# An mLSTM cell and a squared-ReLU FFN on one core: output gates loaded five chunks ahead instead of four

## The chip, the cores and the metric

The kernel runs on one core of a Trainium2 chip. The metric is the device time in microseconds of one execution, as the median of several runs. The engines are named as in the profile: PE (TensorE, with its weight loads PEld), DVE (VectorE), ACT (ScalarE), POOL (GpSimd) and SP (SyncE, which here only issues DMAs). Each engine takes its instructions in the order of the program, and waits for the others by semaphores.

## The reference, cut to what matters

An mLSTM cell runs over 768 steps for 4 batches and 8 heads of 40 elements. Its output, gated by the sigmoid of `o_gate`, is laid out as 3072 tokens of 320 and goes through an FFN.

```
for t in range(S):
    m_new  = maximum(f_gate[t] + m, i_gate[t])
    f_stab = exp(f_gate[t] + m - m_new);  i_stab = exp(i_gate[t] - m_new);  m = m_new
    C = f_stab * C + i_stab * outer(v[t], k[t])
    n = f_stab * n + i_stab * k[t]
    denom = maximum(abs(n . q[t]), 1)
    y[t] = sigmoid(o_gate[t]) * (C @ q[t]) / denom
x = y as (B*S, H*D) = (3072, 320)
h = maximum(x @ w_in, 0)            # 320 -> 2048
out = (h * h) @ w_out               # 2048 -> 320
```

The inputs, among them `o_gate` with its shape (4, 8, 768, 40), are float32.

## The kernel before

**Chunks and groups.** The sequence is cut into chunks of 128 steps: six to a batch, 24 in all, numbered s = 0 to 23. A chunk's attention is done at once for its eight heads: scores of keys and queries, weights from the decays, their product with the values, and a state C carried to the next chunk. Two chunks (256 tokens) make a group g of the FFN, 0 to 11. Both FFN layers are done for most groups with seven block products instead of eight, so that sums of blocks (`sums`, `sums_of_x`) come ahead of the products and sums of results (`ffn1_close`, `ffn2_fast`) after them.

**The order is written by hand.** The program is emitted in the order in which every engine works, without a planner. A prologue does chunks 0 to 5. Then a loop over `parts` (L1091) does the rest. Four parts, `at` = 0 to 3, go with each chunk s from 6 on, and each part holds a quarter of one FFN layer of one group: in the even ones from 8 on a second layer (`ffn2_fast`), in the odd ones from 9 to 25 a first layer (`ffn1_open`, `ffn1_close`). The attention of chunk s is spread over its four parts; after chunk 23 the parts hold only FFN work.

**A chunk's way through memory.** In part 1, `attend_turned(s)` leaves the numerators turned; `store_num(s)` writes them to a scratch tensor in HBM (`num_rows`, L580) and `load_num(s)` reads them back in another layout (four DMAs, L585). In part 2 `normalise_turned(s)` on DVE (L597 to L606) waits for them, takes the denominator, and multiplies by the gated output `og` of the chunk (L603 and L604 read it) into `x_sb`. Then, on SP: `store_rows(s)` writes `x_sb` out (L632), in odd chunks `load_A(s+2)` (L352), then `prefetch(s)`, then `load_rows(s)` reads the rows back turned (four DMAs, L637), then `pair_up(s+3)` (L305, four DMAs). All of these and the stores of the output (L801, L806) stand in SP's one queue.

**The output gates.** `load_o(s)` (L342) reads 160 KB of `o_gate` for chunk s into its place in a tile `og` that holds a run of chunks: (0, 1), (2, 3), and then four to a run: 4 to 7, 8 to 11, 12 to 15, 16 to 19, 20 to 23 (`RUNS`, L288). The pool has two such tiles, so a run's tile takes the buffer of the run before the last: 12 to 15 takes that of 4 to 7, 16 to 19 that of 8 to 11, and so on. It is opened by the load of the run's first chunk (L339, L340). `sigmoid(r)` (L345) works in place on ACT. To keep ACT from changing its table of functions often, the sigmoids come four at a time: in part 3 of every chunk with s % 4 = 3, for the next run (L1153 to L1156). Chunks up to 11 are loaded in the prologue.

**What stands behind the sigmoids on ACT.** In chunks 11, 15 and 19 part 3 goes on with `ffn1_close`, whose first ACT instruction is the relu L907. The next chunk's part 0 is `ffn2_fast(g, 0)`: PE makes a product into the bank X, and ACT copies it out as `m1` (L785). PE's part 1 goes on summing into the same bank X (L789), so it cannot start before this copy.

The loop's `do(f, s)` calls `f(s)` if 0 <= s < 24 (L923).

Of the kernel before, what the change touches and what calls it, by code (L numbers as in the profile page):

```python
# [29 lines left out]
def kernel(  # L30
# [305 lines left out]
    def load_o(s):  # L336
        b, c = divmod(s, NB)
        r, (s0, s1) = next((r, (a, z)) for r, (a, z) in enumerate(RUNS) if a <= s < z)
        if s == s0:  # L339
            st["og", r] = ld.tile([P, 4, H, D], F32, name="og")  # L340
        og = st.setdefault(s, {})["og"] = st["og", r][:, s - s0]
        nc.sync.dma_start(og, o_gate[b, :, c * P : (c + 1) * P, :].rearrange("h p d -> p h d"))  # L342
# [580 lines left out]
    def do(f, s):  # L923
        if 0 <= s < NT:
            f(s)
# [16 lines left out]
    def load_part(s, i):  # L942
        b, c = divmod(s, NB)
        dst, src = load_parts(s)[i]
        nc.sync.dma_start(dst, src[b, :, c * P : (c + 1) * P, :].rearrange("h p d -> p h d"))
# [65 lines left out]
    for u in range(8):  # L1011
        s = 2 + u // 2
# [72 lines left out]

    def prefetch(s):
        do(lambda s: load_part(s, 2), s + 4)
        if 8 <= s < 20:
            load_o(s + 4)

    for n, (which, g, i) in enumerate(parts):  # L1091
        s, at = 6 + n // 4, n % 4
# [80 lines left out]
        if at == 2:  # L1173
            do(lambda s: weigh(s, masked=True), s + 1)
            ffn1_square()
            if n < 4:
                do(turn_kq, s + 1)
                do(scale_q, s + 1)
            if even:
                do(weighted, s + 1)  # L1180
            do(normalise_turned, s)
            do(store_rows, s)
            if s < 7:
                do(load_squares, s + 2)
            else:
                if not even:
                    do(load_A, s + 2)
                prefetch(s)
            do(load_rows, s)
            if s > 6:  # L1190
                do(pair_up, s + 3)
            else:
                do(load_A, s + 2)
# [35 lines left out]
```

## Time and profile before

| what | value |
|---|---|
| median of 3 runs | 514.7 us |
| lowest and highest | 513.06 and 514.84 us |
| span of the profiled execution | 514.0 us |
| mean granted PE clock in it | 0.993 |
| ACT idle before `sigmoid`, until a load of `og` landed | 25.0 us in 3 times, the longest 8.8 |
| loads of `og` | 24 of 160 KB, 3.0 to 6.2 us from issue to landing, median 5.1 |

A line of a timeline gives the start in us from the begin of the span, the duration in us, the engine, the line of the kernel, the operation, the tile written and the tile read, the shapes and the count. In brackets stands how long the engine was idle before it and what ended that. A line of waits gives the engine and what it wanted to do, what it waited for, the total in us, how many times, and the longest. In the table of windows the columns are the stretch, its length, PE's busy time with the number of its instructions, the granted PE clock (1.00 is full speed), the busy share of the DMA engines, and GB/s. SPq is SP's queue of DMA issues: the duration of an issue is not that of the transfer.

### The profile page before, as it was taken

To read this page: it belongs to the slowest core of one execution; us is meant where nothing else is said; L and a number is where in the kernel's file an instruction comes from. 1 tells how busy PE (TensorE), PEld (TensorE's weight loads), DVE (VectorE), ACT (ScalarE), POOL (GpSimd) and SP (SyncE) were. 2 spreads that over 40 slices of the span, in tenths; PEclk is the share of its full clock that TensorE was granted. 3 is DMA by queue.
4 is the path that set the end of the run, shared out by engine and by line. 5 is a ranking of instruction groups with operands and counts; after the bars stand their busy time and mean duration, and the time that the engine had idled before them with its cause. 6 is when DMAs were issued, how large, how long until landed. Compare 5 with 4: busy or idle time off the path is not lost.

```text
span 514.0 us, 13827 instructions
## 1 busy us (share of the span) xinstructions
PE 497.0 (97%) x5640; PEld 460.1 (89%) x5641; DVE 351.5 (68%) x646; ACT 249.3 (49%) x492; POOL 119.9 (23%) x138
## 2 busy tenths in 40 slices
PE   9998989999999999989999989999979999999997
PEld 4867878897799999979999979999979999999997
DVE  8588948979956956647867666587576766645441
ACT  3767878853541650653551743551745550432400
POOL 3356723421332041013023005023004012020000
PEclk9999989999999999989999999999999999999999
DMA  9999897947566757666667677577575541210000
GB/s 190 212 229 205 257 199 141 219 94 144 125 129 149 157 122 145 143 149 127 133 145 146 128 159 150 124 159 148 122 154 117 112 119 49 72 17 27 1 27 26
DMA packets 238238, 67.74 MB, mean 132 GB/s; under 512 B 185600, under 2 KB 232704, under 8 KB 238176
## 3 DMA queue, kind: packets, MB, share of 16 engines
q1 hardware_dynamic: 238080, 66.68, 61.3%
q8 instruction: 44, 0.72, 0.6%
q10 hardware_dynamic: 96, 0.20, 0.1%
q14 instruction: 18, 0.15, 0.1%
HBM read 54.56 MB, written 17.86 MB: 141 GB/s over the span
## 4 chain that ended last, share of the span: by engine, by line
PE 81%; DMA 6%; DVE 6%; ACT 3%; SPq 2%; issue 1%; POOL 0%; DVEq 0%; POOLq 0%; ACTq 0%
PE h_ps L765 31%; PE h_ps L841 22%; PE h_ps L890 6%; PE h_ps L711 3%; DMA og<-in_o_gate_dram 3%; PE numT L551 3%; PE h_ps L674 3%; DMA num_rows<-tn 2%; PE hp L490 1%; SPq L585 1%; PE idle L934 1%; PE tp L453 1%; PE numT L542 1%; DMA kq<-num_rows 1%; PE tp L445 1%
## 5 line engine op out<-in xcount | busy, mean ns | idle before, releaser
L377 POOL TENSOR_SCALAR_AFFINE_SELECT A_bc<-A_bc 128x1024 f32<-128x1024 f32 x22 | 25.9, 1177 | 164.8 <-ACT kq L387 143.5
L765 PE MATMUL h_ps<-w_out,g 128*128 128x160 f32 x336 | 50.8, 309 | 4.2 <-ACT y_sb L785 4.2
L765 PE MATMUL h_ps<-T,S 128*128 128x160 f32 x352 | 51.6, 300 | 2.6 <-DVE g_c L909 1.5
L765 PEld LDWEIGHTS h_ps<-w_out,g 128*128 128x128 f32 x336 | 47.6, 195 | 5.8 <-ACT y_sb L785 4.5
L765 PEld LDWEIGHTS h_ps<-T,S 128*128 128x128 f32 x352 | 48.9, 190 | 3.3 <-issue 1.7
L401 ACT ACTIVATE A_bc<-A_bc,b_T 128x128 f32<-128x128 f32 x144 | 44.1, 388 | 7.0 <-POOL A_bc L377 6.7
L781 DVE TENSOR_TENSOR y_sb<-y_sb,h_ps 128x160 f32<-128x160 f32 x44 | 14.0, 319 | 46.2 <-PE h_ps L765 46.2
L871 ACT COPY r_sb<-h_ps 128x512 f32<-128x512 f32 x18 | 10.5, 585 | 71.3 <-PE h_ps L841 71.3
L841 PE MATMUL h_ps<-xT,w_in 128*128 128x128 f32 x320 | 42.8, 278 | 0.0
L841 PE MATMUL h_ps<-lent_t,w_in 128*128 128x128 f32 x320 | 42.2, 275 | 0.0
L841 PEld LDWEIGHTS h_ps<-xT,w_in 128*128 128x128 f32 x320 | 38.9, 192 | 1.1 <-issue 0.7
L890 PE MATMUL h_ps<-xT,w_in 64*64 64x128 f32 x960 | 39.4, 273 | 0.0
L841 PE MATMUL h_ps<-lent_t 128*128 128x128 f32 x320 | 39.1, 275 | 0.0
L841 PEld LDWEIGHTS h_ps<-lent_t,w_in 128*128 128x128 f32 x320 | 38.9, 192 | 0.0
L841 PEld LDWEIGHTS h_ps<-lent_t 128*128 128x128 f32 x320 | 37.3, 192 | 0.1
L890 PEld LDWEIGHTS h_ps<-xT,w_in 64*64 64x64 f32 x960 | 34.6, 133 | 2.4
L674 PE MATMUL h_ps<-xT,w_in 128*128 128x256 f32 x128 | 30.6, 392 | 1.2 <-POOL w_in L230 0.6
L568 DVE STREAM_TRANSPOSE tn<-numT 128x256 f32<-128x256 f32 x36 | 15.5, 444 | 22.8 <-PE numT L551 22.8
L765 PE MATMUL h_ps<-w_out,g_c 128*128 128x160 f32 x192 | 28.0, 302 | 1.5 <-ACT y_sb L785 1.5
L674 PEld LDWEIGHTS h_ps<-xT,w_in 128*128 128x128 f32 x128 | 24.3, 196 | 5.3 <-POOL w_in L230 1.0
L413 POOL TENSOR_TENSOR vw<-va,A_bc 128x328 f32<-128x328 f32 x15 | 13.4, 892 | 67.2 <-issue 47.0
L765 PEld LDWEIGHTS h_ps<-w_out,g_c 128*128 128x128 f32 x192 | 26.3, 190 | 2.2 <-ACT y_sb L785 1.6
(188 smaller groups left out, 1071.3 us busy)
## 6 DMA issues: line engine op xcount, KB each, us to landing
A_bc<-a_rows SPq DMA_DIRECT2D x22, 512.0 KB, 5.0
num_rows<-tn SPq DMA_DIRECT2D x18, 256.0 KB, 2.5
kq<-num_rows SPq DMA_DIRECT2D x72, 64.0 KB, 2.0
raw<-in_moe_w_out_dram SPq DMA_DIRECT2D x7, 640.0 KB, 4.1
kqT<-kq_rows SPq DMA_DIRECT2D x34, 128.0 KB, 3.2
kq<-in_k_dram SPq DMA_DIRECT2D x24, 160.0 KB, 3.7
va<-in_v_dram SPq DMA_DIRECT2D x24, 160.0 KB, 5.1
og<-in_o_gate_dram SPq DMA_DIRECT2D x24, 160.0 KB, 5.1
```

The lines of the kernel that those rows point to most:

```text
L377: nc.gpsimd.affine_select(A[:], A[:], compare_op=ALU.is_ge, fill=-1e30, base=0, pattern=[[0, H], [1, P]], channel_multiplier=-1,)
L401: nc.scalar.activation(d["W"][:, i * n + h, :], A[i][:, h, :], AF.Exp, bias=b_T[:, b, c, i * n + h : i * n + h + 1],)
L413: nc.gpsimd.tensor_tensor(d["vw"][:], d["va"][:], d["W"][:, :, P - 1 : P].to_broadcast([P, H, D1]), op=ALU.mult,)
L551: nc.tensor.matmul(numT[i][halves[g], e, :], lhsT=va_w[s % NKQ][:, h * D1 : h * D1 + DP], rhs=d["P"][h % 2][:, h // 2, :] if s < KQ_SQ els ...
L568: nc.vector.transpose(to[:, 2 * i : 2 * i + 2], numT[i][:, :2, :].rearrange("p c t -> p (c t)"))
L674: nc.tensor.matmul(hs[i][:, n, :], lhsT=w_in[:, a, fb * P : (fb + 1) * P], rhs=xT[:, :, a, :], start=(n == 0 and a == 0), stop=False,)
L711: nc.tensor.matmul(o_ps, lhsT=st["g2", g][:, fb, j * P : (j + 1) * P], rhs=w_out[:, fb, :], start=(fb == 0), stop=(fb == NF - 1),)
L765: nc.tensor.matmul(to, lhsT=lhsT[:, p], rhs=rhs[:, p, :], start=(start and p == 0), stop=(p == NPAIR - 1), skip_group_check=True,)
L781: add = lambda to, a, b: nc.vector.tensor_tensor(to, a, b, op=ALU.add)
L841: nc.tensor.matmul(to[:, n, :], lhsT=lhsT[:, 4 * q + n, :], rhs=rhs, start=(start and n == 0), stop=True, skip_group_check=True,)
L871: nc.scalar.copy(m1[:], X[:])
L890: nc.tensor.matmul(to[cols, n, :], lhsT=w_in2[rows, 4 * q + n, cols], rhs=rhs, start=(start and n == 0), stop=True, skip_group_check=True,)
```

## The change

`prefetch(s)` is called once in each chunk from 7 on, in part 2, between the store and the load of the chunk's rows. It loads the values for chunk s + 4. Before, it also loaded the output gates of chunk s + 4 in the chunks 8 to 19, so for chunks 12 to 23. After, it loads those of chunk s + 5 wherever there is such a chunk: called in chunks 7 to 18, for the same chunks 12 to 23. Nothing else changes: the sigmoids stay where they are, and so does the number of `og` tiles.

```diff
     def prefetch(s):
         do(lambda s: load_part(s, 2), s + 4)
-        if 8 <= s < 20:
-            load_o(s + 4)
+        do(load_o, s + 5)
```

## The prediction

> **What bounds the kernel now.** I read the page first: the busy row, then the chain that ended last, by engine and by line.
>
> ```profile
> PE 497.0 (97%) x5640; PEld 460.1 (89%) x5641; DVE 351.5 (68%) x646; ACT 249.3 (49%) x492; POOL 119.9 (23%) x138
> ...
> PE 81%; DMA 6%; DVE 6%; ACT 3%; SPq 2%; issue 1%; POOL 0%; DVEq 0%; POOLq 0%; ACTq 0%
> PE h_ps L765 31%; PE h_ps L841 22%; PE h_ps L890 6%; PE h_ps L711 3%; DMA og<-in_o_gate_dram 3%; PE numT L551 3%; PE h_ps L674 3%; DMA num_rows<-tn 2%; PE hp L490 1%; SPq L585 1%; PE idle L934 1%; PE tp L453 1%; PE numT L542 1%; DMA kq<-num_rows 1%; PE tp L445 1%
> ```
>
> PE is the bound, with 17 us of idle time in 514.0; so a gain is PE idle time removed, or PE made faster. The chain has the load of og in it with 3.2% (16.5 us). That is not the gain: while the chain runs through that load, PE works. What the load costs PE is in PE's own waits, taken from 96 us on (the loop of parts):
>
> ```profile
> PE h_ps L765 <- ACT y_sb L785: 5.7, 3, 2.5
> PE h_ps L765 <- DVE g_c L909: 1.5, 1, 1.5
> PE h_ps L765 <- DVE g L909: 1.2, 2, 0.7
> ```
>
> Three waits for the copy L785, 5.7 us, and three for L909, 2.7 us. The timelines of ACT and of SP around the first place (chunk 11) say why ACT is late:
>
> ```profile
> 212.06 1.28 ACT L345 ACT_TABLE_LOAD   x1
> 213.35 1.19 ACT L345 ACTIVATE og<-og 128x320 f32<-128x320 f32 x3
> 222.85 0.47 ACT L345 ACTIVATE og<-og 128x320 f32<-128x320 f32 x1 [8.31 <-DMA og<-in_o_gate_dram]
> 223.22 0.58 ACT L907 ACTIVATE g<-h_ps 128x512 f32<-128x512 f32 x1
> 223.70 0.28 ACT L785 COPY y_sb<-h_ps 128x160 f32<-128x160 f32 x1
> ```
> ```profile
> 197.07 1.06 SPq L342 DMA_DIRECT2D og<-in_o_gate_dram  x1
> ...
> 215.35 0.38 SPq L632 DMA_DIRECT2D x_rows<-x_sb  x1
> ...
> 217.03 0.82 SPq L342 DMA_DIRECT2D og<-in_o_gate_dram  x1
> ```
>
> Three sigmoids run at once; the fourth, og(15), is issued only at 217.03, lands 5.8 us later, and ACT stands 8.31 us with the relu L907 and the copy L785 behind it. PE at the three places (chunks 11, 15, 19):
>
> ```profile
> 224.04 6.20 PE L765 MATMUL h_ps<-w_out,g 128*128 128x160 f32 x32 [2.52 <-ACT y_sb L785]
> ...
> 303.39 4.61 PE L765 MATMUL h_ps<-w_out,g_c 128*128 128x160 f32 x32 [1.52 <-ACT y_sb L785]
> ...
> 381.56 4.61 PE L765 MATMUL h_ps<-w_out,g 128*128 128x160 f32 x32 [1.70 <-ACT y_sb L785]
> ```
>
> The same 32 products take 6.20 us at the first place and 4.61 at the others. The windows of PE show the reason, the granted clock (column after the busy time):
>
> ```profile
> 223.50:224.00 0.50, 0.00 (x0) 0.88 0.56 76
> 224.00:225.00 1.00, 0.96 (x4) 0.50 0.44 129
> ...
> 226.00:227.00 1.00, 1.00 (x6) 0.50 0.95 312
> 227.00:227.50 0.50, 0.50 (x5) 0.71 0.91 162
> 227.50:228.00 0.50, 0.50 (x6) 1.00 0.76 136
> ```
>
> Half clock for 3.4 us, right after the longest of the three gaps.
>
> **What the Trainium skill says.** "TensorE: Matmul & The Clock Gate", Part 1 (What's actually happening): PE's clock is halved after a window of about 3.4 us (3413 ns) with little activity, and the window runs freely, so whether a gap triggers it depends on its phase. The trace agrees in length (3.4 us at 0.50), and the shorter gaps of 1.52 and 1.70 us left the clock at 1.00. The same page (Architectural detail) calls ACT a strict FIFO; the trace agrees, L907 starting 0.37 us after the late sigmoid. "Perfetto Trace Analysis", DMA Instruction — HWDGE: an issue's duration leaves out the movement of data; here 0.82 us of issue against 5.8 us to landing.
>
> **The change part by part.** Before, prefetch(s) loads og(s+4); sigmoid(12..15) stands in chunk 11, part 3, one part after og(15) is issued; likewise chunks 15 and 19. After, og(15) is issued where og(14) was, at 197.07, and lands at about 202, ten microseconds before the sigmoids begin at 213.35.
>
> ACT: the fourth sigmoid follows the third at about 214.5, ends at 215.0, L907 (0.58) by 215.6, and L785 runs when its product ends (213.79 + 2.44 = 216.2), so by 216.6. PE wants that bank at 221.5 (224.04 - 2.52): 5 us to spare. At the other places the product ends at 295.9 and 373.1, PE comes at 301.9 and 379.9: the wait goes whole. PE saves 2.52 + 1.52 + 1.70 = 5.74 us. These lie on the bound engine with nothing beside them.
>
> Clock: without the 2.52 us gap the halved window at 223.9 has no cause: 6.20 - 4.61 = 1.59 us more. From below it is worth 0 (a run whose window fell otherwise); from above 1.7 (3.41 us at half clock). I take 1.6. A second such window, about 67 to 70.4 us (mean clock 0.84 from 60 to 70), lies before the loop; I leave it in.
>
> What PE meets next: the second product of the step writes the bank that DVE's L781 reads; L781 comes after L760, done at 221.17, so by 221.5, and PE needs it at 221.5 + 2.2. No wait. The three L909 waits hang on normalise_turned waiting for num_rows, not on og: they stay.
>
> SP: 12 loads before, in chunks 8 to 19; 12 after, in chunks 7 to 18, each at the same place in the queue. Only the ends differ. Chunk 7 gains an issue (0.65 median): SP waits there for 0.64 us anyway (va issued until 138.19, xT's load from 138.83, for x_rows to land), and later for DVE's L574 before L580, 1.6 us; 0. The 160 KB beside xT's loads may stretch these by up to 0.9 us (they take 4.0 there, 4.4 to 4.9 where og goes ahead): hidden by the same wait. Chunk 19 loses an issue of 0.82 us, before work with slack: 0, at best -0.9.
>
> New wait: in chunks 7, 11 and 15 the load opens a tile over the buffer of the run that ends in that very chunk, so it needs normalise_turned(s) to have read it. The last read, L604, ended at 214.6; SP's store of x_rows at 215.35, just ahead, has already waited for the later L606. So the wait is met on arrival; 0, or the 0.02 to 0.05 us that SP's small pieces take in the chain. Behind it stand four xT loads, pair_up's four and store_num(s+1); DVE's next normalise waits for the last.
>
> Sum: 5.74 + 1.59 = 7.3 us; 514.0 becomes 506.7 by the profiled span. The three timed runs give 514.7 in the middle, 0.7 more; with the same difference 507.4.
>
> **The rivals.**
> Only the gaps (0.20): the median run had no halved window at that place. The times speak for it a little (513.06 to 514.84, a spread of one such window), the profiled execution against. 514.7 - 5.74 = 509.0.
> Another wait takes part of it (0.07): store_num(12) follows pair_up on SP at 225.06 whatever PE does, so its rows do not come earlier. They land near 231.1 (229.1 + 2.0) and normalise(12) would start at 236.05 - 4.1 = 231.9: 0.8 us spare; in chunk 16, 313.05 against 314.85 - 1.5: 0.3 us. If DVE comes late there and PE's banks with it, half of 5.74 returns: 514.7 - 2.9 - 1.6 = 510.2. Against it: DVE's work there is not what PE waits for next.
> More (0.07): the early halved window (1.6) or part of the L909 waits (2.7) goes too, about 2.4 of the 4.3: 505.0.
> Nothing (0.02): the sigmoid waits for something else than the load that is moved; the wait's name speaks against it. 514.7.
> Slower (0.04): the reused buffer is given free not by L604 but by something in the next chunk, so SP stands in its queue in chunks 7, 11 and 15. It decides from about 5 us of hold (normalise(12) at 236.05 against rows at 231.1). A hold of 9 us, to L568 of the next chunk, costs 3 x 4 = 12 us against 7.3 gained: 519.4. Against it: L604 is the last reader that the code has.
> The forecast: 0.60, with its own range 506.2 to 508.6.
>
> **How the numbers follow.** The likeliest case gives 507.4. The range takes in the case of the gaps alone and most of the case of more: 505.5 to 510.0, leaving out half of those at either end, nothing and slower, under 0.2. A measurement of this kernel tells about 0.5%, 2.6 us, from no change. Faster by more: 0.60 + 0.20 + 0.07 + 0.07 = 0.94; within: 0.02; slower: 0.04.
>
> **What would show it.** Right: no idle time of ACT before og, L785 before 217, no wait of PE for L785, PE's 32 products at 4.6 us in chunk 12, clock 1.00 there, L909's waits as before, og no more in the chain. Wrong: SP idle before L342 in chunk 7, 11 or 15; a new PE wait in chunks 12, 16 or 20; or a halved window somewhere else in the loop, which gives the 1.6 us back.

## The result, and the profile after

| | before | after |
|---|---|---|
| median of 4 runs | 514.77 us | 508.12 us |
| lowest and highest | 513.06 to 514.97 | 507.12 to 508.66 |
| ratio, with its 95% interval | | 0.9876 [0.9848, 0.9904] |
| span of the profiled execution | 514.0 us | 506.9 us |
| mean granted PE clock in it | 0.993 | 0.997 |

The change made the kernel faster by 6.65 us; the forecast said 7.3 us less and 507.4. Ratios and intervals, here and below, leave out the executions that took over 1.5% longer than the fastest of their kernel. The page of the changed kernel, in the lines that answer to those shown of before:

```profile
PE 494.5 (98%) x5640; PEld 458.7 (90%) x5641; DVE 352.0 (69%) x646; ACT 250.0 (49%) x492; POOL 122.4 (24%) x138
...
PE 94%; DVE 2%; issue 1%; ACT 1%; DMA 1%; POOL 0%; SPq 0%; DVEq 0%; POOLq 0%
PE h_ps L765 34%; PE h_ps L841 25%; PE h_ps L890 8%; PE h_ps L674 4%; PE numT L551 4%; PE h_ps L711 3%; PE hp L490 2%; PE h_ps L445 2%; PE tp L445 2%; PE numT L542 1%; PE idle L934 1%; PE h_ps L685 1%; PE tp L453 1%; PE dC L483 1%; PE dC L561 1%
```

The load of og is gone from the chain, which is now 94% PE. PE's busy time fell by 2.5 us with the same 5640 matmuls, its idle time from 17.0 to 12.4 us. ACT's timeline at the end of chunk 11 shows the mechanism as forecast: four sigmoids in a row, no idle time ahead of them, and the copy L785 at 214.06 after a wait for its own product only.

```profile
211.15 1.55 ACT L345 ACTIVATE og<-og 128x320 f32<-128x320 f32 x4
212.60 0.57 ACT L907 ACTIVATE g<-h_ps 128x512 f32<-128x512 f32 x1
214.06 0.29 ACT L785 COPY y_sb<-h_ps 128x160 f32<-128x160 f32 x1 [0.88 <-PE h_ps L765]
```

PE's waits, again from 96 us on, are all new ones. Neither L785 nor L909 is among them:

```profile
PE h_ps L445 <- PE h_ps L765: 2.6, 3, 0.9
PE h_ps L445 <- issue: 1.6, 1, 1.6
```

L445 is the product of `scores(s+1)`, in part 1 of an even chunk; the four waits are in chunks 14, 16, 18 and 20 (0.93, 0.94, 0.74 and 1.60 us). The releasers named ("PE", "issue") are not the cause; what PE waits for is found on PE's and DVE's timelines. First PE, at the three places of the old waits or near them:

```profile
218.49 4.61 PE L765 MATMUL h_ps<-w_out,g 128*128 128x160 f32 x32
...
292.95 1.11 PE L445 MATMUL h_ps<-kqT 40*64 40x128 f32 x29 [0.94 <-PE h_ps L765]
...
370.07 1.23 PE L445 MATMUL h_ps<-kqT 40*64 40x128 f32 x29 [1.60 <-issue]
```

The 32 products in chunk 12 take 4.61 us instead of 6.20. But ahead of the scores there are now gaps, 0.94 us in chunk 16 and 1.60 in chunk 20. DVE's timeline just ahead of the second:

```profile
364.64 0.17 DVE L597 TENSOR_SCALAR dm<-kq 128x8 f32<-128x8 f32 x1 [4.34 <-DMA kq<-num_rows]
...
366.35 0.68 DVE L908 TENSOR_TENSOR r_sb<-r_sb,h_ps 128x512 f32<-128x512 f32 x1
...
368.74 1.24 DVE L334 STREAM_TRANSPOSE kqT<-kqT 128x1024 f32<-128x1024 f32 x1
```

DVE waited 4.34 us for the numerator rows of chunk 19 (`load_num`), then worked without a pause through `normalise_turned`, L908 to L911 and `turn_kq` (L334). That ends at 369.98, and PE starts `scores` on its result at 370.07. The windows of PE after the gap (columns as in the earlier table of windows):

```profile
370.00:371.00 1.00, 0.93 (x30) 0.97 1.14 261
371.00:374.00 3.00, 3.00 (x43) 0.50 0.76 112
374.00:374.50 0.50, 0.50 (x20) 0.65 0.11 20
374.50:375.00 0.50, 0.50 (x13) 1.00 0.55 154
```

Half clock again for 3.4 us (370.9 to 374.3), now in chunk 20.

**Where the time went, by the two profiles.** The loop, from the first numerator product of chunk 6 to the end, took 514.0 - 107.6 = 406.4 us before and 506.9 - 105.4 = 401.5 after: 4.9 us less. Of this 4.2 is idle time of PE (gaps over 0.1 us from 100 us on: 8.4 before, 4.2 after). The other 2.2 us of the 7.1 lie in the prologue, which the change does not touch; there before had the halved window near 67 us that the prediction had left in, and after had none. So the total agrees with the forecast better than its parts do. That is why both kernels were run again.

### The profile page after: what moved, and what is told of

It is laid out like the page before. It is cut to its first block, busy times and chain, and to the rows that moved or that the text cites. A ratio compares the mean times of both kernels' runs of the same rounds, so it can differ in the third digit from the quotient of the medians.

```text
span 506.9 us, 13821 instructions
## 1 busy us (share of the span) xinstructions
PE 494.5 (98%) x5640; PEld 458.7 (90%) x5641; DVE 352.0 (69%) x646; ACT 250.0 (49%) x492; POOL 122.4 (24%) x138
## 4 chain that ended last, share of the span: by engine, by line
PE 94%; DVE 2%; issue 1%; ACT 1%; DMA 1%; POOL 0%; SPq 0%; DVEq 0%; POOLq 0%
PE h_ps L765 34%; PE h_ps L841 25%; PE h_ps L890 8%; PE h_ps L674 4%; PE numT L551 4%; PE h_ps L711 3%; PE hp L490 2%; PE h_ps L445 2%; PE tp L445 2%; PE numT L542 1%; PE idle L934 1%; PE h_ps L685 1%; PE tp L453 1%; PE dC L483 1%; PE dC L561 1%
## 5 line engine op out<-in xcount | busy, mean ns | idle before, releaser
L765 PE MATMUL h_ps<-w_out,g 128*128 128x160 f32 x336 | 49.2, 303 | 0.0
L765 PEld LDWEIGHTS h_ps<-w_out,g 128*128 128x128 f32 x336 | 46.1, 190 | 1.4 <-issue 1.2
L387 ACT ACTIVATE kq<-A_bc 64x512 f32<-64x512 f32 x30 | 18.8, 626 | 18.8 <-DMA A_bc<-a_rows 18.6
L908 DVE TENSOR_TENSOR r_sb<-r_sb,h_ps 128x512 f32<-128x512 f32 x20 | 13.7, 684 | 20.7 <-PE h_ps L841 14.3
```

Source lines behind the costliest of these rows:

```text
L387: nc.scalar.activation(e[rows], st[s]["A"][0][rows, PR * i : PR * (i + 1), :], AF.Exp)
L765: nc.tensor.matmul(to, lhsT=lhsT[:, p], rhs=rhs[:, p, :], start=(start and p == 0), stop=(p == NPAIR - 1), skip_group_check=True,)
```

## The experiments

Each ratio is to the kernel before, run beside it on the same chip, since that median was 511.8 to 512.6 us in the later sets. The median is of all executions of a run. "L785" and "L445" are PE's waits so named from 96 us on, in the one profiled execution. Those of e4 and e11 took 511.66 and 514.26 us, long for their kernels, so their waits are less certain. The cuts of e4 and e7 are against the kernel before, all others against the changed kernel.

| run | median us | ratio, 95% interval | L785 | L445 |
|---|---|---|---|---|
| e1 before, again | 511.71 | 0.9983 [0.9963, 1.0004] | 5.4 | 0.4 |
| e2 after, again | 509.81 | 0.9933 [0.9904, 0.9961] | 0 | 4.3 |
| e3 last load only | 506.72 | 0.9879 [0.9833, 0.9924] | 0 | 1.6 |
| e4 sigmoid later | 508.63 | 0.9920 [0.9894, 0.9947] | 0 | 3.7 |
| e5 first run only | 510.31 | 0.9957 [0.9931, 0.9983] | 2.1 | 0.3 |
| e6 other runs only | 510.56 | 0.9954 [0.9932, 0.9976] | 2.2 | 3.2 |
| e7 PE kept busy | 512.44 | 0.9984 [0.9955, 1.0013] | 0.6 | 0.4 |
| e8 normalise late | 510.05 | 0.9952 [0.9928, 0.9976] | 0 | 4.2 |
| e9 pairs in even chunks | 505.29 | 0.9874 [0.9829, 0.9919] | 0 | 0.7 |
| e10 pairs in odd chunks | 508.35 | 0.9926 [0.9896, 0.9955] | 0 | 3.7 |
| e11 after, third time | 507.97 | 0.9920 [0.9902, 0.9938] | 0 | 5.3 |
| e12 values in even chunks | 504.45 | 0.9872 [0.9829, 0.9916] | 0 | 1.1 |

The runs e1 to e4, e5 to e8 and e9 to e11 were each made on one chip, e12 by itself. In e7 the added line shifts L785 to L786.

**e1 and e2: the two kernels unchanged.** What of the gain is there again on another chip?

> The kernel before once more, nothing changed, to see how many halved-clock windows each of its executions has. Each window takes 0.0033 off the mean granted clock (3.41 us at half speed in 514) and should add some 1.6 us. Theory A (windows come by chance, by the phase of the gaps): the executions differ in clock by steps of 0.0033 and in time by steps of 1.6 us; most have one in chunk 12 and one near 68 us, 514.7 in the middle. Rival (the windows belong to the kernel): clock 0.993 and the same time in all.

> The changed kernel once more. Theory A: 508.1 in the middle, clocks of 0.993 to 1.000 in steps of 0.0033, the higher the shorter the span. If the windows play no part in the spread, span and clock are not related.

The waits repeat: e1 has the three for L785 with 5.4 us, e2 has none and 4.3 us at L445 instead. The gain is smaller than in the first measurement: 0.9933, about 3.4 us, its interval just touching the first one's. The mean clock of an execution comes in steps of about 0.0033 (0.997, 0.993, 0.990, 0.987), and one stretch of 3.41 us at half clock in 510 us is such a step: 3.41 x 0.5 / 510 = 0.0033. Counted so, an execution has from none to five windows. On this chip the kernel before has 2.14 on average in the 22 executions of e1 and 2.48 in the 48 that ran beside all four runs, the changed kernel 2.50 in 18. Across the executions of a chip, the time rises by 1.15 ± 0.16, 1.48 ± 0.12 and 1.18 ± 0.20 us per window on the three chips. So the average price is somewhat below the 1.6 of the prediction, and no fall in the number can be seen.

This count has a weakness. The traces tell the place of each window, and of the 28 in the 14 profiled executions 21 lie at 40 to 74 us, in the prologue, which no run touches. In the loop there are seven: one in each of the two profiles of the kernel before, one in two of the three profiles of the changed kernel, one in e5 and two in e4. If these profiles are typical, the count says little of the loop, and the price is mainly that of a window in the prologue.

**e3: only the last load of each run.** Load og(15), og(19) and og(23) in chunks 10, 14 and 18; leave the others. That takes ACT's wait away with 3 loads moved in place of 12.

```diff
-        do(load_o, s + 5)
+        if 8 <= s < 20 and s % 4 < 3:
+            load_o(s + 4)
+            if s % 4 == 2:
+                load_o(s + 5)
```

> Only the last load of each run (og of chunks 15, 19, 23) goes one chunk earlier, into chunks 10, 14 and 18, behind the load that stands there; the other nine loads stay where they were. Theory A (the late landing of these three alone held ACT): no idle time of ACT before a sigmoid, no PE wait for L785, 508.1 as the changed kernel, within 1 us. Rival B (the order of the loads as a whole, or the issue added in chunk 7, matters): between 508 and 514.7. Doubling the issue in chunks 10, 14, 18 may cost SP 0.9 us each, which should be hidden.

It is faster than the changed kernel in the same set, 506.72 against 509.81. PE waits 1.6 us at L445 where e2 waits 4.3, and its loop takes 397.1 us against 400.2. So moving these three loads is enough for the benefit, and where SP has its loads matters for the rest: e3 takes the three out of odd chunks (11, 15 and 19) into even ones, while the change leaves six og loads in odd chunks as before.

**e4: the sigmoid later, the loads unmoved.** The fourth sigmoid goes into part 1 of the next chunk, behind the copies; no DMA is moved.

```diff
-                for r in range(s + 1, min(s + 5, NT)):
+                for r in range(s + 1, min(s + 5 if s < 11 else s + 4, NT)):
                     sigmoid(r)
...
             do(attend_turned, s)
+            if s > 11 and s % 4 == 0:
+                do(sigmoid, s + 3)
             do(decays, s + 1)
```

> All loads stay as in the kernel before (og(s+4)); instead the fourth sigmoid of the runs 12-15, 16-19 and 20-23 moves on ACT, from chunk 11, 15, 19 part 3 to chunk 12, 16, 20 part 1, behind the copy L785 and just ahead of the decays, where no further table load is needed. Theory A (the order on ACT is all that matters, the load itself hinders nobody): as the changed kernel, 508 to 509, no PE wait for L785, ACT idle before the fourth sigmoid at most about 1 us. Rival B (the gain comes from moving the loads): 514.7.

The ratio is 0.9920, as e11 has it for the whole change. The wait at L785 is gone, and 3.7 us come up at L445. The loads land late as before, but behind the copies they hold ACT up for little:

```profile
ACT og L345 <- DMA og<-in_o_gate_dram: 3.0, 3, 1.2
```

So the order on ACT is the cause of the old waits, and not the load as such. And the wait at L445 comes up here too, with all loads where they were: it is not made by the moved loads alone, it appears when PE gets there earlier.

**e5 and e6: one part of the change alone.** e5 moves the loads of og(12) to og(15), e6 those of og(16) to og(23).

```diff
 e5:
-        do(load_o, s + 5)
+        if s < 11:
+            load_o(s + 5)
+        elif 12 <= s < 20:
+            load_o(s + 4)
 e6:
-        do(load_o, s + 5)
+        if 8 <= s < 12:
+            load_o(s + 4)
+        if 11 <= s < 19:
+            load_o(s + 5)
```

> Only the loads of the run 12-15 go one chunk earlier (issued in chunks 7 to 10); those of 16 to 23 stay. Theory A: the PE wait for L785 of 2.5 us in chunk 12 goes and those of 1.5 and 1.7 us in chunks 16 and 20 stay; also the halved window that followed the longest gap: 2.5 to 4.1 us, 510.6 to 512.2. Rival C (each place only hands its time to the next): less than 1 us.

> Only the loads of the runs 16-19 and 20-23 go one chunk earlier (from chunk 11 on); those of 12 to 15 stay. Theory A: the waits of 1.5 and 1.7 us in chunks 16 and 20 go, the 2.5 us and its halved window in chunk 12 stay: 3.2 us, 511.5; with the run of place 1 the two gains sum to that of the whole change. What PE waits for behind normalise in chunks 15 and 19 stays and may show at L445 rather than at the product before it.

e5 gains 2.2 us (0.9 to 3.5 by its interval) and e6 2.4. The first place is worth about its gap of 2.52; a window's 1.6 on top, 4.1 in all, lies outside the interval. In e6 the wait at L445 comes up (3.2 us), as its expectation had it, in e5 hardly (0.3). Together the two are worth 0.0089, within what the whole change measured in its three sets (0.0067 to 0.0124). In e6 the first place keeps its wait, and its line on PE's timeline has the 32 products at full speed all the same:

```profile
222.49 4.61 PE L765 MATMUL h_ps<-w_out,g 128*128 128x160 f32 x32 [2.22 <-ACT y_sb L785]
```

No window at half clock follows it. So the 2.5 us of gap that the prediction called the window's cause makes one possible, not certain.

**e7: fill the gaps with work.** In the kernel before, the state products dC of chunks 12, 16 and 20 are done six, four and four times, with the same result, so that PE runs while it would wait.

```diff
+        for again in range({12: 6, 16: 4, 20: 4}.get(s, 1)):
             (the loop of dC products, indented)
```

> The kernel before, with PE's gaps of chunks 12, 16 and 20 filled: the 16 matmuls into dC are done six, four and four times (each pass about 0.41 us and with the same result), in the time in which PE would wait for L785. The waits stay as long in sum (gap and filling together), so no gain from them. Theory A (the halved window of chunk 12 comes from the idle time): clock 1.00 in chunk 12 in every execution, mean clock 0.997 to 1.000, about 1.6 us or less gained, 513 to 514. Rival (the window does not come from the gap): a window in chunk 12 as before, 514.7.

The windows are 1.77 on average against 2.09 of before in the same set, a difference of 0.32 ± 0.24, so that a fall is not shown; the profiled execution has none in the loop. The time, 0.9984 [0.9955, 1.0013], is not told from no change: 0.3 windows of 1.15 to 1.5 us would be 0.4 to 0.5 us, less than the interval can tell. What the gap's window is worth at this place stays open.

**e8: normalise behind L908 to L911.** If the wait at L445 came from DVE's order, with the transposition queued behind the late normalise, then the L908 group ahead of normalise should shorten it. The changed kernel, with `normalise_turned` and what follows it put behind `ffn1_close` in odd chunks:

```diff
-        if at == 2:
+        if at == (3 if fast and s > 8 else 2):
             do(normalise_turned, s)
```

> The changed kernel, and in the odd chunks from 9 on normalise_turned with all that follows it (the store and load of the rows, prefetch, pair_up) is emitted after ffn1_close of part 3 instead of before it, so that on DVE L908 to L911 stand ahead of the normalise, which waits about 4 us for num_rows. In the changed kernel PE waits 4.2 us in four places for the transpose L334 that stands behind these. Theory D (DVE's late turn_kq, held up by the wait for num_rows, is the rest of PE's idle time): the waits at L445 shrink, by up to 1.2 us each, 504 to 507. Rival (L334 waits for its own load, kqT): as the changed kernel, 508, or slower, since the rows go out 1.5 us later.

L445 stays at 4.2. Now the transposition has rows of its own to wait for:

```profile
DVE kqT L334 <- DMA kqT<-kq_rows: 7.5, 5, 1.9
```

Both the numerator rows and `kqT` come through SP's queue, one after the other. So a better order on DVE alone brings nothing here. The run does not acquit DVE's order by itself, since it also sends all that follows the normalise on SP out later; e9 and e12, which leave DVE's order as it is, show that the queue alone can take most of the wait away.

**e9 and e10: in which chunks SP has the loads.** e9 and e10 load two og at a time, e9 in even chunks, e10 in odd ones.

```diff
 e9:
-        do(load_o, s + 5)
+        if 8 <= s < 20 and s % 2 == 0:
+            load_o(s + 4)
+            load_o(s + 5)
 e10:
-        do(load_o, s + 5)
+        if s < 19 and s % 2:
+            load_o(s + 5)
+            load_o(s + 6)
```

> The same twelve loads, none of them in an odd chunk: the even chunks 8 to 18 load og(s+4) and og(s+5). Each load is issued at latest one chunk before its sigmoids, so PE should not wait for L785. Theory E (what PE still waits for at L445 in the changed kernel, 4.2 us, comes from SP's queue, which in the odd chunks has A_bc, va, og and xT in a row and is late with the next num_rows and kqT): the waits at L445 fall to 0 to 2 us, the loop from the first numT to the end takes 397 us or less, against 401.5 and 400.2 in the two profiles of the changed kernel; 505 to 507. Rival F (the waits come from the num_rows round trip itself, whatever else SP has to do): as the changed kernel, waits of 4 us.

> The other way round: all twelve loads in odd chunks, two in each of 7 to 17: og(s+5) and og(s+6). Again every load lands long before its sigmoid: no PE wait for L785. Theory E: SP is later by one more issue (0.8 to 2.2 us) in the odd chunks 9 to 17 and less loaded in 19; the waits at L445 grow to 5 to 9 us, so most of the change's gain is gone, 510 to 514. Rival F: as the changed kernel, waits of 4 us.

e9 waits 0.7 us at L445 and takes 505.29 us, 2.7 us less than the changed kernel in the same set (e11, 507.97). e10 was expected to have 5 to 9 us of the wait and has 3.7, no more than the changed kernel. The direction of e9 holds, the dose of e10 does not: a second load in the odd chunks does no further harm once the even ones have none. SP's timelines say in part why. From the store of the rows of an odd chunk (L632, chunks 11 to 17) to the next `store_num` it is 10.1 us on average in the changed kernel, 8.6 in e9 and 11.1 in e10; after the store of an even chunk (12 to 18) it is 9.9, 9.2 and 9.4. So e10 gets back in the even chunks half of what it loses in the odd ones, and the two together take 20.0, 17.7 and 20.5 us. That this sum decides fits the three kernels; it was not tested by itself.

**e11: the changed kernel once more**, beside e9 and e10.

> The changed kernel for the third time, beside the two variants on the same chip. Ratio to the kernel before between the two measured, 0.988 and 0.993; waits at L445 of about 4 us in sum, none for L785.

The ratio is 0.9920, a gain of 4.0 us, with no wait at L785 and 5.3 us at L445.

**e12: the same with another tensor.** The changed kernel, with the loads of the values va (of the same kind, on the same queue) taken out of the odd chunks. If SP's queue is the cause, it does not matter which load leaves it.

```diff
     def prefetch(s):
-        do(lambda s: load_part(s, 2), s + 4)
+        if s % 2 == 0:
+            do(lambda s: load_part(s, 2), s + 3)
+            do(lambda s: load_part(s, 2), s + 4)
         do(load_o, s + 5)
```

> The changed kernel (og loads in every chunk, odd ones too), but the loads of the values, 160 KB each as well, are taken out of the odd chunks: the even chunks 8 to 20 load va(s+3) and va(s+4). Theory E in the form that the runs so far leave (SP reaches store_num late in odd chunks because of what it has to issue before, whichever tensor it is): the issue of store_num in chunks 13, 15, 17, 19 comes at most 4 us after PE's last matmul into numT, instead of 4.6 to 5.4, and the waits at L445 fall from 4.2 to 0 to 2 us; 505 to 507. If it is the gates' own load, the waits stay at 4 us and the time at that of the changed kernel.

The median is 504.45 us, the ratio 0.9872, and PE waits 1.1 us at L445. SP's timelines in chunks 17 to 19 show how. First the changed kernel:

```profile
346.49 0.93 SPq L801 DMA_DIRECT2D out_dram<-y_sb  x1
347.51 0.39 SPq L632 DMA_DIRECT2D x_rows<-x_sb  x1
...
357.12 0.38 SPq L580 DMA_DIRECT2D num_rows<-tn  x1
...
360.20 2.90 SPq L585 DMA_DIRECT2D kq<-num_rows  x4
```

and e12:

```profile
342.83 0.53 SPq L801 DMA_DIRECT2D out_dram<-y_sb  x1
344.86 0.36 SPq L632 DMA_DIRECT2D x_rows<-x_sb  x1
...
354.51 0.38 SPq L580 DMA_DIRECT2D num_rows<-tn  x1
...
357.20 1.75 SPq L585 DMA_DIRECT2D kq<-num_rows  x4
```

In e12 SP is done with L801 at 343.4 and stands until the rows of chunk 18 are ready, at 344.86; in the changed kernel it goes straight on, comes to this store late, and so to everything after it: `store_num` of chunk 19 (L580) and its rows (L585). From this store to DVE's start on the rows of chunk 19 it is 17.1 us in the changed kernel (347.51 to 364.64) and 17.3 in e12 (344.86 to 362.20), so the gain lies ahead of the store: there the stretch from the rows of an odd chunk to the next `store_num` is 8.4 us on average in place of 10.1. The waits of SP's queue show the same slack over the loop (105 to 400 us), in the kernel before, in the changed kernel and in e12:

```profile
SPq L632 <- DVE y_sb L781: 11.8, 5, 3.6
```
```profile
SPq L632 <- DVE y_sb L781: 4.6, 3, 2.3
```
```profile
SPq L632 <- DVE y_sb L781: 13.3, 7, 2.7
```

It is 13.7 in e9 and 8.5 in e3, but 1.6 in e10, where PE waits no longer than in the changed kernel; so it shows where SP stops, and does not measure PE's wait. DVE's wait for `num_rows` (L597) over the same stretch goes with PE's: 21.3 us in the changed kernel and 22.1 in e10, 11.6 in e9 and 15.0 in e12 (before, where PE itself came later, 16.6). The issue of `store_num` comes after PE's last numerator product by 4.6, 5.3, 5.0 and 5.4 us in chunks 13, 15, 17 and 19 of the changed kernel, by 3.8, 3.4, 3.1 and 3.8 in e12. The end of the path in chunk 20 of e12 is PE at L445, with 0.20 us of gap in place of 1.60:

```profile
367.64 1.11 PE L445 MATMUL h_ps<-kqT 40*64 40x128 f32 x29 [0.20 <-PE h_ps L765]
```

And DVE's wait for the rows ahead of it is 2.92 us in place of 4.34, 1.42 less, as the gap is 1.40 less.

## Why the prediction was right, point by point

**ACT and L785: right.** The 5.74 us of waits are gone in the changed kernel and in every variant that gives ACT its last load or its last sigmoid a place that suits it (e3, e4, e9, e10, e12); e5 still has one of those that it leaves, and e6 the first.

**The clock: mis-sized.** The window in chunk 12 went (4.61 us against 6.20), and one in chunk 20 came, after a gap of 1.60 us. That is the prediction's own "a halved window somewhere else in the loop, which gives the 1.6 us back". On average no fall is seen: 2.14 and 2.48 windows in the two sets of the kernel before on one chip, 2.50 after. So nothing in the runs shows the 1.59: neither these counts, which are mostly of the prologue, nor e5, whose gain is that of the gap alone. The price of a window was right within 0.1 to 0.45 us as an average over all places; that the number falls was not. What one window in the loop costs was not measured apart.

**What PE meets next, and the L909 waits: failed.** The prediction said that PE, on leaving the gap, meets no further wait, and that the L909 waits, 2.7 us, stay. Instead these vanished and 4.2 us at L445 came: the "new PE wait in chunks 12, 16 or 20" that it names as a sign of being wrong. The two kinds are the same lateness: DVE waiting for `num_rows`. It was there before (4.15 us for chunk 19, 4.34 after), and PE met it one product earlier. Before, in chunk 20, and then after:

```profile
374.57 2.41 PE L765 MATMUL h_ps<-T,S 128*128 128x160 f32 x16 [1.48 <-DVE g_c L909]
```
```profile
366.13 2.34 PE L765 MATMUL h_ps<-T,S 128*128 128x160 f32 x16
366.94 0.68 DVE L909 TENSOR_TENSOR g_c<-r_sb,h_ps 128x512 f32<-128x512 f32 x1
```

After, the same product begins before L909 does, and waits for a semaphore of ACT in place of DVE's. So it seems to take an accumulator bank that ACT's L907 frees, and not the one that L909 frees; the bank itself stands in no trace. PE passes on to `scores`, and there waits for L334. The step that failed is the rival's refutation, "DVE's work there is not what PE waits for next": it is, by way of L334. The spare times that the rival works out, 0.8 and 0.3 us, are for the rows of chunks 12 and 16; the late rows were those of 13, 15, 17 and 19. The net loss, 4.2 less the 2.6 us of waits for L909 before, is 1.6 us; the rival had put it at half of 5.74, 2.9. It is about what PE waits in chunks 14 and 18 (0.93 and 0.74 us), where it did not wait before.

**SP at no cost: failed, by the same amount.** The moved loads cost nothing where the prediction looked, at L342: SP does not stand ahead of any, so no wait for the buffer shows. But the queue as a whole had only as much slack as PE's own waits left it (11.8 us before and 4.6 after, at the store of the rows). Once PE runs 5.7 us faster through three chunks, SP cannot follow, and taking a load out of the odd chunks helps it (e9, e12). A kernel with another buffer for og was not tried; that no wait for the buffer matters rests on the trace alone.

**The sum.** 5.74 less 1.6 of new waits, and nothing for the clock, gives 4.1 us. The repeats measured 3.4 and 4.0 us, and the loops of the five profiles (406.4 and 405.7 us before; 401.5, 400.2 and 403.1 after) differ by 4.4 on average. The first measurement had 6.65: there the kernel before took 514.77 us, and 511.7 to 512.6 in all later sets, while the changed kernel took much the same (508.12; 509.81 and 507.97). Why is not known. In its profiles 2.2 us of the difference lie in the prologue, which the change does not touch (it stands the other way round between e1, 105.6 us, and e2, 106.8). It happened to fill the place of the 1.6 that the prediction had for the clock and of the 1.6 of new waits that it left out. The forecast of the time was right by this luck as much as by its reasons. Taken as gains, "another wait takes part of it" (4.5 us) came closer to the repeats than "only the gaps" (5.7): it named the right mechanism, and only the argument against it was wrong. Nothing, and slower by a held buffer, did not occur.

**Open:** whether the loads hold SP by their issue alone or also by slowing what SP waits to see land, since every variant moves both; whether the sum over two chunks explains e10; what the halved clock at the first place was worth in time (e7); and how much of the rest of the loop (0.7 us between the two profiles) is chance.

## What to carry to other kernels

Take the gain from the bound engine's own waits, and then ask of each wait removed which queue had slack only because of it: here SP, and it gave back 1.6 of 5.7 us. Where a load can stand in one of two kinds of chunk, put it in the one in which the queue stops anyway: the same loads in even chunks (e9), or another tensor's (e12), brought 1.3% against 0.7% to 0.8% for the change in its repeats. (e12 ran without the changed kernel beside it; e9 beat it by 2.7 us in the same set.) Compare halved-clock windows over many executions, and find out first in which part of the kernel they lie.

## What the runs showed of the hardware that was not expected

The granted clock is halved in windows of 3.41 us, from none to five in an execution of this kernel, at 1.15 to 1.48 us each on average. In the traces' records of the clock, all its changes within one execution lie whole multiples of 3.413 us apart: before, windows begin at 66.869 and 223.882 us, 46 multiples apart, and in e11 at 66.875 and 377.487, 91 apart. This agrees with the free-running window that the prediction quotes from the Trainium skill ("TensorE: Matmul & The Clock Gate", What's actually happening). That section has the clock fall after an idle window of about 3.4 us; here it fell after a gap of 1.60 us in one execution and 2.52 in another, and not after 2.22 us in e6, so that shorter gaps can be enough. What decides it stays open.

An issue's duration on SP's queue is not fixed: the og load in chunk 11 takes 0.82 us before and 2.08 after, and the four xT loads behind it 4.44 and 2.92, so 5.3 and 5.0 us together. One issue alone gives no price; the sum with its neighbours does.
